# The up products of the first layer's last two token blocks as one Strassen pair, with their weight sums prepared from block 1 on

## The chip, the cores and the metric

The kernel runs on one core of a Trainium2 chip. The metric is device time in microseconds (us) of one execution, the median over runs. The kernel before takes 1470.53 us (three runs, 1470.46 to 1470.94). All operands lie in HBM in float32 and the output is float32. A core has five engines: TensorE (PE, matrix products into PSUM), VectorE (DVE), ScalarE (ACT), GpSimd (POOL) and SyncE (SP), which here issues nearly all DMA transfers. Each engine works through its own instructions in the order in which they were written.

## The reference, cut to what matters

```python
kv  = einsum('bhsd,bhse->bhde', k, v)            # B, H, S, D = 8, 8, 576, 64
o   = einsum('bhsd,bhde->bhse', q, kv)           # no softmax
x   = o / sqrt(mean(o*o, -1) + 1e-6) * g_norm    # -> 4608 tokens x 512

h   = maximum(maximum(x @ w1, x @ w2), x @ w3)   # first layer: 512 -> 768
x   = h @ w_out                                  # 768 -> 512

xn  = x / sqrt(mean(x*x, -1) + 1e-6) * rms_g     # second layer
g   = xn @ w_gate                                # 512 -> 1536
out = (g * sigmoid(g) * (xn @ w_val)) @ w_out2   # 1536 -> 512
```

## The kernel before

**Numbers.** A float32 operand is kept as two parts, hi (rounded to the fast fp32r format) and lo (the rest), and each product is three matmuls, hi x hi, hi x lo and lo x hi, of 128 rows against 512 tokens. Every operand is made so first: hi by ACT (a copy), lo by DVE or POOL (a subtraction).

**Tiles.** The 4608 tokens are nine blocks of 512 (`TB`), a block four token groups (`NS`), and the 512 features four slices of 128 (`KC`). The first layer has six hidden columns of 128 (`J1`), the second twelve (`J2`).

**Order.** The start, up to block 1, follows a written list (`ORDER`). After it the program is loops: for each block `t` and hidden column `j`, `do_p` makes the three up products of the column (each four slices of three matmuls; the maximum is taken by ACT, DVE, DVE), and `do_o` the column's down product (`acc`). Between them stands `slot()`: it runs the work planned for this slot with `at(n, fn)`, a step of the last block's norm (`flush`), a step of the sums of a token pair (`aside`), and one step of the weight preparation (`prep`). The attention of the block ahead is cut into steps as well (`token`: po, sq, ss, pw, xn, pt, hi, lo), five slots to a token group. `pt` is a transpose on PE, and it reads what `xn` on DVE wrote.

**Second layer.** Block 0 is computed directly (`do_gv`, then `do_o`). Blocks 1 to 8 go as four pairs, each by Strassen's scheme in Winograd's form: seven products in the place of eight (`run_unit`, `down`). It needs sums of weight quarters and of token quarters. The weight sums are made in blocks 2 to 8 by 18 `Prep`s, each of 15 steps, from the raw 64-bit words over a float conversion (`conv_a`, `sign`, `conv_bits`, lines 108 to 119) and the sums (lines 209 to 212) to hi and lo (`ws`); four tiles of each are stored to HBM (`wd`), to be loaded again later. `pair_sums` does the same for a pair's tokens (`td`).

**Pools.** `unit` takes one of 38 tiles of 128 x 1024 values: weights, hidden columns and everything in preparation; `room` limits how many of them the preparation may hold (`live`). `psum` takes one of four PSUM banks (`ps`), and `acc` one of four others (`pa`).

Of the kernel before, what the change touches and what calls it, by code (L numbers as in the profile page):

```python
# [20 lines left out]
P = 128  # L21
# [38 lines left out]
def tile_kernel(ctx: ExitStack, tc, qT, k, v, kvt0, kvt1, w1, w2, w3, wo, wg, wv, wo2, out):  # L60
# [97 lines left out]
    class Prep:  # L158

        def __init__(self, i, jp):
# [12 lines left out]
        def step(self):  # L175
            need, fn = self.steps[self.n]
            if live[0] + need > room[0] and need > 0:
                return
            live[0] += need
            if fn:  # L180
                fn()
            self.n += 1

        def load(self, i, jp):
            self.tt, self.g = [], []
# [46 lines left out]

    preps = []
    wait = []

    def prep():
# [5 lines left out]
        if wait and (not preps or len(preps) < 2 and preps[-1].n >= 8) and live[0] + 2 <= room[0]:  # L242
# [17 lines left out]
    def load_kv_part(b, c, only=None):  # L260
        r = b * S
        m, tail = KV.setdefault(b, ([None] * 4, []))
        if c == 2:
# [9 lines left out]
            else:  # L273
                for i, src in enumerate((k, v)):
                    tail.append(rp.tile([P, 512], F32, tag="raw", name="kvt")[:64])
# [83 lines left out]
    def token_steps(i, pool=ps):  # L359
# [42 lines left out]
        def hi():  # L402
            if i // NS not in X:
                new_x(i // NS)
            nc.scalar.activation(X[i // NS][:, 0, :, cut_of(i)], st["pt"], AF.Copy, scale=gc)

        def lo():
            x = X[i // NS]
            f = cut_of(i)
            nc.vector.scalar_tensor_tensor(x[:, 1, :, f], st["pt"], gc, f32(x[:, 0, :, f]), ALU.mult, ALU.subtract)  # L410
# [388 lines left out]
    def slot():  # L799
# [3 lines left out]
        if not side or n_slot[0] % 2:  # L803
            prep()

# [243 lines left out]
    with tc.manual_schedule():  # L1049
# [36 lines left out]
        for word in ORDER.split():  # L1086
# [53 lines left out]
        wait += [Prep(i, jp) for jp in range(J2 // 2) for i in range(3)]  # L1140
        for j in range(J1 - 1):
# [6 lines left out]
        for t in range(2, NB):  # L1148
            last = t + 1 == NB
            if not last:  # L1150
# [7 lines left out]
                if t + 2 < NB:  # L1158
                    at(19, lambda i=base // 2 + 2: load_q(i))
# [4 lines left out]
            else:  # L1164
                at(3, lambda: new_x(NB))
                for c in range(KC):
                    at(4 * c, lambda c=c: load_x2(c))
                    at(4 * c + 4, lambda c=c: hi_x2(c))
                    at(4 * c + 5, lambda c=c: lo_x2(c))
            for j in range(J1):  # L1170
# [8 lines left out]
                if last and j > 2:  # L1179
                    load_w2(j - 3)  # L1180
                if last and j == 3:
                    load_wo2(0)
                slot()
        while preps or wait:
            slot()


        xb = None
        for j in range(J2):
            if j % 2 == 0 and j + 2 < J2:  # L1190
                load_wo2(j // 2 + 1)
            if j + 3 < J2:
                load_w2(j + 3)
# [4 lines left out]
            do_gv(NB, j, slot)  # L1198
            slot()
            if j == 0:  # L1200
                do_o(1, NB - 1, J1 - 1, J1)
# [78 lines left out]
```

## Time and profile before

| | |
|---|---|
| time, median of three runs | 1470.53 us (1470.46 to 1470.94) |
| the profiled execution's own time | 1469.55 us |
| its span, first instruction to last | 1467.4 us |
| PE busy, matmuls | 1459.8 us, 99% of the span, 7262 matmuls |
| DVE, ACT, POOL busy | 62%, 42%, 29% of the span |
| DMA moved | 316.16 MB, a mean of 215 GB/s |

The page cuts the span into 40 slices; PE is at nine tenths or more in each but the first. The chain that ended last is followed back from the last instruction, at each step to what released it; its shares say which engine set the end.

### The profile page before, as it was taken

What the parts mean: (1) busy time and instruction counts of PE and PEld (TensorE: products, weight loads), DVE (VectorE), ACT (ScalarE), POOL (GpSimd) and SP (SyncE); (2) the same over time, 40 slices, a digit from 0 to 9 for tenths busy, and PEclk for the clock granted to TensorE, in tenths of its full rate; (3) what the DMA queues carried; (4) which work ended last, traced back from release to release, by engine and by line L of the source; (5) the groups of instructions that cost most, each with busy time, mean ns of one, the idle gap of its engine ahead of it and who ended that gap; (6) DMA issues with size and microseconds to landing.
All of it is one profiled execution on the core that took longest, in us unless ns stands there. A gap on an engine that the chain in (4) does not pass through costs nothing.

```text
span 1467.4 us, 19952 instructions
## 1 busy us (share of the span) xinstructions
PE 1459.8 (99%) x7262; PEld 1214.7 (83%) x7262; DVE 908.5 (62%) x1377; ACT 620.2 (42%) x1095; POOL 425.3 (29%) x311
## 2 busy tenths in 40 slices
PE   8999999999999999999999999999999999999999
PEld 8888888888888888888888888888888888888887
DVE  6863566676677757752445475674765655754756
ACT  6863354445453545442224342343343442433422
POOL 3212222222231213211232332632424422433323
PEclk9999999999999999999999999999999999999999
DMA  9421435565556662749687654784757843775542
GB/s 362 156 93 58 138 129 194 194 243 210 193 208 251 223 236 108 259 176 391 221 295 269 233 192 173 292 333 152 278 198 275 309 188 149 287 289 198 187 175 105
DMA packets 107218, 316.16 MB, mean 215 GB/s; under 512 B 12977, under 2 KB 13233, under 8 KB 107121
## 3 DMA queue, kind: packets, MB, share of 16 engines
q1 hardware_dynamic: 99200, 302.95, 55.6%
q10 hardware_dynamic: 7920, 11.95, 2.5%
q8 instruction: 57, 0.93, 0.3%
q14 instruction: 41, 0.33, 0.1%
HBM read 241.44 MB, written 73.42 MB: 215 GB/s over the span
## 4 chain that ended last, share of the span: by engine, by line
PE 98%; DMA 1%; SPq 0%; issue 0%; DVE 0%
PE ua L808 18%; PE p L431 10%; PE p L433 10%; PE p L432 10%; PE ub L808 9%; PE da L808 9%; PE db L808 4%; PE uc L808 4%; PE acc L431 4%; PE acc L432 4%; PE acc L433 4%; PE dc L808 2%; PE po L372 2%; PE pk L323 1%; PE pt L400 1%; DMA kvt<-in_kvt 1%
## 5 line engine op out<-in xcount | busy, mean ns | idle before, releaser
L431 PE MATMUL p<-x,w 128*128 128x512 f32 (+1 forms) x656 | 258.1, 393 | 0.0
L433 PE MATMUL p<-x,w 128*128 128x512 f32 (+1 forms) x656 | 254.0, 387 | 0.0
L432 PE MATMUL p<-x,w 128*128 128x512 f32 (+1 forms) x656 | 253.7, 387 | 0.0
L808 PE MATMUL ua<-xo,w 128*128 128x512 f32 x864 | 213.4, 389 | 0.0
L808 PEld LDWEIGHTS ua<-xo,w 128*128 128x128 f32 x864 | 162.2, 188 | 33.7
L450 POOL TENSOR_TENSOR ho<-sl,ho 128x512 fp32r<-128x512 f32 x72 | 97.7, 1364 | 303.9 <-issue 263.6
L450 POOL TENSOR_TENSOR ho<-t,ho 128x512 fp32r<-128x512 f32 x96 | 123.8, 1293 | 132.7 <-ACT ho L449 118.2
L450 POOL TENSOR_TENSOR hs<-h,hs 128x512 fp32r<-128x512 f32 x45 | 67.6, 1502 | 315.2 <-ACT hs L449 295.2
L808 PE MATMUL ub<-xo,w 128*128 128x512 f32 x576 | 146.2, 389 | 0.0
L433 PEld LDWEIGHTS p<-x,w 128*128 128x128 f32 x656 | 123.2, 188 | 25.6
L431 PEld LDWEIGHTS p<-x,w 128*128 128x128 f32 x656 | 123.3, 188 | 24.0 <-issue 0.3
L432 PEld LDWEIGHTS p<-x,w 128*128 128x128 f32 x656 | 123.4, 188 | 23.7
L808 PEld LDWEIGHTS ub<-xo,w 128*128 128x128 f32 x576 | 108.1, 188 | 22.4
L890 ACT ACTIVATE s<-ua 128x512 f32<-128x512 f32 x96 | 57.1, 595 | 139.4 <-PE ua L808 139.1
L808 PE MATMUL da<-ho,wd 128*128 128x512 f32 x432 | 105.7, 389 | 0.0
L449 ACT ACTIVATE ho<-t 128x512 fp32r<-128x512 f32 x96 | 59.4, 627 | 100.5 <-DVE t L641 100.5
L391 POOL TENSOR_TENSOR rs<-ms,mhalf 128x8 f32<-128x8 f32 x36 | 64.6, 1807 | 116.4 <-DVE ms L387 111.5
L462 DVE TENSOR_TENSOR s<-p,s 128x512 f32<-128x512 f32 x45 | 31.1, 691 | 105.5 <-PE p L433 100.4
L808 PEld LDWEIGHTS da<-ho,wd 128*128 128x128 f32 x432 | 81.1, 188 | 16.8
L449 ACT ACTIVATE hs<-h 128x512 fp32r<-128x512 f32 x45 | 28.4, 632 | 139.4 <-DVE h L466 134.5
L431 PE MATMUL acc<-hs,w 128*128 128x512 f32 x216 | 85.4, 395 | 0.0
L838 DVE TENSOR_TENSOR c<-uc,s 128x512 f32<-128x512 f32 x48 | 33.1, 690 | 84.1 <-PE uc L808 83.9
(152 smaller groups left out, 2731.6 us busy)
## 6 DMA issues: line engine op xcount, KB each, us to landing
w<-wd SPq DMA_DIRECT2D x180, 512.0 KB, 7.6
wd<-ws SPq DMA_DIRECT2D x72, 512.0 KB, 3.0
wd<-wd SPq DMA_DIRECT2D x72, 512.0 KB, 7.1
wq<-wd SPq DMA_DIRECT2D x72, 256.0 KB, 8.1
xo<-td SPq DMA_DIRECT2D x32, 512.0 KB, 9.7
q<-in_qT SPq DMA_DIRECT2D x18, 512.0 KB, 6.1
raw<-in_w SPq DMA_DIRECT2D x18, 512.0 KB, 10.1
raw<-in_wo SPq DMA_DIRECT2D x18, 512.0 KB, 6.4
```

Source lines behind the costliest of these rows:

```text
L323: nc.tensor.matmul(pk[h * D:(h + 1) * D, hp, :], kk, vv, start=(c == 0 and hp in ((0, NP // 2) if b == 0 else (0,))), stop=(c == 4), skip_ ...
L372: nc.tensor.matmul(po[:n, f], q[:, hp, o:o + n], kvbd[b][:, hp, :], start=True, stop=True)
L391: nc.gpsimd.tensor_tensor(st["rs"], st["ms"], mhalf.to_broadcast([P, H]), ALU.pow)
L431: nc.tensor.matmul(o, ah, bh, start=first, stop=False)
L432: nc.tensor.matmul(o, ah, bl, start=False, stop=False)
L433: nc.tensor.matmul(o, al, bh, start=False, stop=last)
L449: nc.scalar.activation(hs[:, 0], h, AF.Copy)
L450: nc.gpsimd.tensor_tensor(hs[:, 1], h, f32(hs[:, 0]), ALU.subtract)
L462: nc.vector.tensor_tensor(s2, p, s1, ALU.max)
L808: nc.tensor.matmul(o, aa, bb, start=first and q == 0, stop=last and q == 2, skip_group_check=True)
L838: nc.vector.tensor_tensor(t, p, s, ALU.add)
L890: nc.scalar.activation(t, p, AF.Copy)
```

## The change

The up products of blocks 7 and 8 of the first layer, which were made one block at a time (6 columns x 3 products x 12 matmuls for each block), are made together: the two blocks and the two halves of the features form a 2 x 2 matrix of tokens, and for each of the three up weights columns `j` and `j + 3` form the other. Nine units (`up_unit`) of seven products, six matmuls each, take their place. Around them:

- `Sums`: nine preparations that form the weight sums of the first layer from weights already in SBUF and store them (`sd`). They wait in the same list as the `Prep`s, ahead of them, and begin at the end of block 1, with room for four tiles.
- `prep()` may hold three preparations at once (`depth`, `lead`), looks ahead at the tiles that a preparation will need (`peak`), and is run a second time in every other slot of blocks 2 to 6 (`fast`).
- `tokens_ahead`: in blocks 5 and 6 the attention of blocks 6, 7 and 8 is made early; then the token sums of the pair (`full`, `x_diff`, `x_hi`, `x_lo`).
- `out_down`, `in_down`: the six down weights of the first layer go to HBM and come back, so that their tiles are free meanwhile.
- `Sring`: the weight sums are loaded again, three ahead and then two for each unit.
- `down7` and `down8` make the down products of the two blocks, one block after the other, and layer 2's block 0 follows with two preparation steps a slot (`twice`) and a wait for weights not yet stored (`ready`).

The diff, cut to its core:

```diff
+        lead = 15, 8, 5
         def step(self):
             need, fn = self.steps[self.n]
-            if live[0] + need > room[0] and need > 0:
+            if self.n == 4 and n_slot[0] < self.loaded + 5:
+                return
+            if need > 0 and live[0] + need + (0 if self is preps[0] else preps[0].peak()) > room[0]:
                 return
...
+    class Sums(Prep):
+        lead = 7, 3, 2
+        def __init__(self, i, j):
+            self.n, self.key, self.g, self.loaded = 0, (i, j), [], -9
+            self.steps = [
+                (2, self.fulls), (0, None), (-1, self.diffs), (1, lambda: self.up(0)), (1, lambda: (self.down(0), self.up(1))),
+                (-2, lambda: (self.out(0), self.down(1))), (-1, lambda: self.out(1)),
+            ]
+        def fulls(self):
+            i, j = self.key
+            self.f, self.c = unit([P, 2, 512], F32, "wt"), unit([P, 2, 2, 256], F32, "wt")
+            for n in range(2):
+                w = W[1, i, j + 3 * n]
+                nc.vector.tensor_tensor(self.f[:, n], f32(w[:, 0]), f32(w[:, 1]), ALU.add)
+        def diffs(self):
...
+            nc.vector.tensor_tensor(c0[:, 0], a21, a22, ALU.add)
+            nc.vector.tensor_tensor(c0[:, 1], c0[:, 0], a11, ALU.subtract)
+            nc.vector.tensor_tensor(c1[:, 0], a11, a21, ALU.subtract)
+            nc.vector.tensor_tensor(c1[:, 1], a12, c0[:, 1], ALU.subtract)
+        def up(self, n):
+            self.g.append(unit([P, 2, 2, 256], F32R, "ws"))
+            nc.scalar.activation(self.g[n][:, :, 0], self.c[:, n], AF.Copy)
+        def down(self, n):
+            g = self.g[n]
+            nc.vector.tensor_tensor(g[:, :, 1], self.c[:, n], f32(g[:, :, 0]), ALU.subtract)
+        def out(self, n):
...
+            nc.sync.dma_start(d, f32(self.g[n]))
...
-        if wait and (not preps or len(preps) < 2 and preps[-1].n >= 8) and live[0] + 2 <= room[0]:
+        if wait and not hold[0] and (not preps or len(preps) < depth[0] and preps[-1].n >= preps[-1].lead[depth[0] - 1]) and live[0] + 2 + (preps[0].peak() if preps else 0) <= room[0]:
...
             prep()
+        if fast[0] and not side and n_slot[0] % 2:
+            prep()
...
+        wait += [Sums(i, j) for j in range(J1 // 2) for i in range(3)]
+        room[0], depth[0] = 4, 3
         def pumped():
             tick()
             flush()
+            prep()
...
+        def quarter(u, c, p, s=None):
...
+                    nc.scalar.activation(r, p, AF.Copy)
+                else:
+                    add(p, s, r)
+                return
+            r = R[j, c]
+            if s is not None:
+                p = add(p, s, tmp("c"))
+            nc.vector.tensor_tensor(r, p, r, ALU.max)
+            if i == 2:
...
+                defer(lambda: HT.__setitem__(key, split_h(r, "hs")), 1)
...
+        def up_unit(i, j, between=None):
...
+            b = psum([P, TB], "vb")
+            up1(u, 5, b, True)
+            s5 = copy("s5", b)
+            half_slot()
+            if between is None:
+                c11()
+            up1(u, 6, a)
+            s2 = copy("s2", a)
+            sr.load()
+            half_slot()
+            up1(u, 3, b)
+            quarter(u, 1, b, s2)
+            half_slot()
+            if last1():
+                half_slot()
+            up1(u, 7, a)
+            quarter(u, 3, a, s5)
+            sr.load()
+            half_slot()
+            prev1.append(u)
...
+        depth[0], fast[0] = 3, True
-        for t in range(2, NB):
+        for t in range(2, PA):
...
+                tokens_ahead(t)
...
+        for j in range(J1 // 2):
+            for i in range(3):
...
+                if (i, j) == (1, 0):
+                    room[0], depth[0] = 8, 2
+                if (i, j) == (2, 1):
+                    for n in range(3):
+                        in_down(n)
+                if (i, j) == (0, 2):
+                    for n in range(3, J1):
+                        in_down(n)
+                if (i, j) == (1, 2):
+                    load_w2(0)
+                if (i, j) == (2, 2):
+                    load_w2(1)
                     load_wo2(0)
...
+                up_unit(i, j, between)
...
+            down7(n, n == 0, n == J1 - 1)
...
+            down8(c)
```

How the instructions stand is shown at two places. The first is DVE in block 2. Of the kernel before, from the norm's second `q` rows (`q <- q`, line 541) to the `xn` that a transpose waits for; `ws` and `wt` are tiles of a `Prep`:

```order
L227 TENSOR_TENSOR ws<-wt,ws 128x2x256
L108 TENSOR_SCALAR wt<-raw 128x512
L385 TENSOR_REDUCE ss<-sq 128x8
L387 TENSOR_SCALAR ms<-ss 128x8
L549 TENSOR_TENSOR two<-q,two 128x512
L227 TENSOR_TENSOR ws<-wt,ws 128x2x256
L108 TENSOR_SCALAR wt<-raw 128x512
L227 TENSOR_TENSOR ws<-wt,ws 128x2x256
L118 TENSOR_SCALAR wt<-wt 128x512
L119 ISA wt<-wt 128x1024
L462 TENSOR_TENSOR s_1997<-p_1984,s_1973 128x512
L349 TENSOR_TENSOR xn<-po,rs 128x512
```

The same place of the changed kernel, its end, from `two` to the same `xn` (now line 401); L265 to L268 are the four lines of `diffs`, and L276 is the lo part of a sum:

```order
L610 TENSOR_TENSOR two<-q,two 128x512
L265 TENSOR_TENSOR wt<-wt 128x256
L266 TENSOR_TENSOR wt<-wt 128x256
L267 TENSOR_TENSOR wt<-wt 128x256
L268 TENSOR_TENSOR wt<-wt 128x256
L276 TENSOR_TENSOR ws<-wt,ws 128x2x256
L265 TENSOR_TENSOR wt<-wt 128x256
L266 TENSOR_TENSOR wt<-wt 128x256
L267 TENSOR_TENSOR wt<-wt 128x256
L268 TENSOR_TENSOR wt<-wt 128x256
L276 TENSOR_TENSOR ws<-wt,ws 128x2x256 x2
L523 TENSOR_TENSOR s_2091<-p_2078,s_2059 128x512
L401 TENSOR_TENSOR xn<-po,rs 128x512
```

Ahead of this piece, between the `h` of the column before and `two`, stand one more group L265 to L268, one more L276 and four `fulls` (L260, `wt <- w`, in two pairs), besides `x`, two `q`, `ss` and `ms`, which are the same in both kernels. So from that `h` to this `xn` the changed kernel has 4 `fulls`, 12 `diffs` and 4 `ws` where the one before had 3 `ws` and the four conversions L108 (two), L118 and L119.

The second place is SP's queue of transfers while blocks 7 and 8 are in work. Of the kernel before, in block 7, where the token sums of blocks 5 and 6 are stored (`td`, from the tiles `th`, `b` and `y`); `raw` is a load of raw weights:

```order
L231 DMA wd<-ws 128x1024
L658 DMA td<-th 128x512
L659 DMA td<-b 128x512
L658 DMA td<-th 128x512
L659 DMA td<-y 128x512
L231 DMA wd<-ws 128x1024
L102 DMA raw<-in_wo 128x1024 x2
```

Of the changed kernel, in the same work on blocks 5 and 6, now in the middle of the nine units (line 1263 is `Sring`'s load, 1416 the load of `in_down`, 240 the store of a `Prep`):

```order
L1263 DMA w<-sd 128x1024 x2
L719 DMA td<-th 128x512
L720 DMA td<-b 128x512
L1416 DMA w<-od 128x1024 x3
L719 DMA td<-th 128x512
L720 DMA td<-y 128x512
L240 DMA wd<-ws 128x1024
L1263 DMA w<-sd 128x1024
```

The preparation and the token sums store as before, and the loads of the weight sums and of the down weights now stand in the same queue between them.

## Rows read from the trace of the kernel before

**Rows 1.** The page: the span, and each engine's busy time with its share and instructions.

```profile
span 1467.4 us, 19952 instructions
...
PE 1459.8 (99%) x7262; PEld 1214.7 (83%) x7262; DVE 908.5 (62%) x1377; ACT 620.2 (42%) x1095; POOL 425.3 (29%) x311
```

**Rows 2.** The page: the chain that ended last, shares of the span by engine.

```profile
PE 98%; DMA 1%; SPq 0%; issue 0%; DVE 0%
```

**Rows 3.** PE's waits in the whole span: us in total, times, longest.

```profile
PE busy L298 <- POOL mhalf L1053: 1.4, 1, 1.4
PE pt L400 <- DVE xn L349: 1.2, 3, 0.7
PE pk L323 <- DMA kvt<-in_kvt: 0.8, 1, 0.8
PE po L372 <- ACT kvbd L332: 0.7, 1, 0.7
```

**Rows 4.** The same chain in order of time, Strassen pairs: start us, us, what.

```profile
788.18 1.36 PE ub L808 x6
789.54 1.36 PE uc L808 x6
```

**Rows 5.** Timeline of DVE in block 2: start us, us, line, operation, [idle before <-releaser].

```profile
191.69 0.69 DVE L466 TENSOR_TENSOR h<-p,s 128x512 f32<-128x512 f32 x1 [4.59 <-PE p L433]
...
192.96 2.38 DVE L541 TENSOR_TENSOR q<-q 128x512 f32<-128x512 f32 x2
195.26 0.68 DVE L227 TENSOR_TENSOR ws<-wt,ws 128x512 fp32r<-128x512 f32 x1
195.86 0.41 DVE L108 TENSOR_SCALAR wt<-raw 128x512 f32<-128x512 f32 x1
...
198.21 0.42 DVE L108 TENSOR_SCALAR wt<-raw 128x512 f32<-128x512 f32 x1
...
199.14 0.41 DVE L118 TENSOR_SCALAR wt<-wt 128x512 int32<-128x512 int32 x1
199.59 0.69 DVE L119 CUSTOM_DVE_ANT_0 wt<-wt 128x1024 uint16<-128x1024 uint16 x1
201.18 0.69 DVE L462 TENSOR_TENSOR s<-p,s 128x512 f32<-128x512 f32 x1 [0.89 <-ACT wt L114]
201.78 0.68 DVE L349 TENSOR_TENSOR xn<-po,rs 128x512 f32<-128x512 f32 x1
...
206.16 0.42 DVE L209 TENSOR_TENSOR wt<-wt 128x256 f32<-128x256 f32 x1
206.61 0.43 DVE L210 TENSOR_TENSOR wt<-wt 128x256 f32<-128x256 f32 x1
206.96 0.42 DVE L211 TENSOR_TENSOR wt<-wt 128x256 f32<-128x256 f32 x1
```

**Rows 6.** The chain in the same stretch: the transpose that reads the last xn.

```profile
204.29 0.44 PE pt L400 x4
```

**Rows 7.** Timeline of POOL in the same stretch.

```profile
193.12 1.66 POOL L450 TENSOR_TENSOR hs<-h,hs 128x512 fp32r<-128x512 f32 x1 [10.21 <-ACT hs L449]
197.22 1.95 POOL L391 TENSOR_TENSOR rs<-ms,mhalf 128x8 f32<-128x8 f32 x1 [2.43 <-DVE ms L387]
```

**Rows 8.** Busy us (instructions) of PE, PEld, DVE, ACT, POOL; clock, DMA share, GB/s.

```profile
130.00:630.00 500.00, 500.00 (x2725) 416.52 (x2724) 335.86 (x565) 234.51 (x420) 119.72 (x75) 1.00 0.54 193
```

**Rows 9.** The same columns, three stretches of 10 us at full DMA share.

```profile
660.00:670.00 10.00, 10.00 (x46) 8.29 (x45) 1.98 (x3) 1.23 (x2) 1.29 (x1) 1.00 1.03 415
730.00:740.00 10.00, 10.00 (x45) 8.26 (x45) 7.91 (x8) 1.83 (x4) 4.92 (x4) 1.00 1.03 388
780.00:790.00 10.00, 10.00 (x46) 8.29 (x45) 3.96 (x6) 4.65 (x8) 0.00 (x0) 1.00 1.02 366
```

**Rows 10.** DMA issues: tiles, queue, count, KB each, median us from issue to landing.

```profile
w<-wd SPq DMA_DIRECT2D x180, 512.0 KB, 7.6
wd<-ws SPq DMA_DIRECT2D x72, 512.0 KB, 3.0
```

More of the change, by code (lines that the diff above doesn't have):

```diff
@@ L182, in step, with peak @@
             self.n += 1
+        def peak(self):
+            have = [sum(x for x, _ in self.steps[self.n:n + 1]) for n in range(self.n, len(self.steps))]
+            return max(have + [0])
         def load(self, i, jp):
+            self.loaded = n_slot[0]
             self.tt, self.g = [], []
@@ new lines, in x_units, with __init__, load @@
+        def x_units():
+            X[PA] = [unit([P, 2, TB], F32R, "x") for _ in range(KC)]
+        class Sring:
+            def __init__(self):
+                self.todo = [(i, j, g) for j in range(J1 // 2) for i in range(3) for g in (1, 2)]
+                self.have = {}
+            def load(self):
+                if self.todo:
+                    key = self.todo.pop(0)
+                    w = self.have[key] = unit([P, 2, 2, 256], F32R, "w")
+                    nc.sync.dma_start(f32(w), sd[key])
@@ new lines, in tile_kernel, with half_slot, last1, down7 @@
+        n_half = [0]
+        def half_slot():
+            n_half[0] += 1
+            if n_half[0] % 2:
+                tick()
+            else:
+                slot()
+        prev1 = []
+        def last1():
+            if prev1:
+                u = prev1.pop()
+                up1(u, 4, u["a"])
+                quarter(u, 2, u["a"])
+                return True
+        DA = {}
+        def down7(j, first=False, last=False):
+            if first:
+                DA[PA] = [pa.tile([P, DM], F32, tag="acc", name="acc") for _ in range(NS)]
+            h, w = HT.pop((PA, j)), W[1, "o", j]
+            for c in range(KC):
+                f = slice(c * P, (c + 1) * P)
+                mm3(DA[PA][c], w[:, 0, f], w[:, 1, f], h[:, 0], h[:, 1], first, last)
@@ new lines, in down8 @@
+        def down8(c):
+            d = psum([P, DM], "acc8")
+            f = slice(c * P, (c + 1) * P)
+            for j in range(J1):
+                h, w = HT[PB, j], W[1, "o", j]
+                mm3(d, w[:, 0, f], w[:, 1, f], h[:, 0], h[:, 1], j == 0, j == J1 - 1)
+            if c % 2 == 0:
+                DA["u"] = unit([P, 2, TB], F32, "y8")
+            y = DA["u"][:, c % 2]
+            DA.setdefault(PB, []).append(y)
+            nc.scalar.activation(y, d, AF.Copy)
+        od = {}
@@ L1209, in tile_kernel @@
                 slot()
+            if j == 1:
+                load_x(1)
             if j == 2:
```

219 lines of the change are left out of this document (197 added, 22 removed).

## The prediction

> **What bounds the kernel now.** I read the page's busy shares first, then the chain, then PE's waits, and only then the engines beside PE. The span is 1467.4 us, and PE's matmuls alone are busy for 1459.8 of it [rows 1]. The chain that ended last runs through PE for 98%; DMA has 1%, all of it at the start [rows 2]. PE's waits that are listed come to 4.1 us, none longer than 1.4 [rows 3]. So after the start PE never stands still, and time leaves this kernel only with matmuls. Nothing else can gain; DVE, ACT, POOL and the transfers can only lose, by making PE wait. The profiled execution took 1469.55 us, 2.15 outside its span, and lies 0.98 under the median of 1470.53. I sum the changes against the profiled execution and add 0.98 at the end.
>
> **Removed.** A product of six matmuls stands in the chain with 1.36 us, one behind the other [rows 4], which is 226.7 ns a matmul. Before, blocks 7 and 8 had 2 x 6 x 3 x 12 = 432 up matmuls. After, nine units of seven products of six make 378. The down products stay (6 x 12 and 4 x 18 groups of three as before, only in another order), and no other matmul is added. So 54 x 226.7 ns = **12.2 us** leave PE. This term is sure. It is the whole gain, and the rest of the sum is what PE newly waits for.
>
> **Added on DVE in block 2 (the weight sums).** Here the order shows 4 `fulls`, 12 `diffs` and one more `ws` between an `h` and the `xn` that a transpose on PE waits for. What stands there has little slack. From its timeline, `h` starts at 191.69 and `xn` ends at 201.78 + 0.68 = 202.46 [rows 5]; the transpose that reads it starts at 204.29 [rows 6]. Slack: 1.83 us. Prices: operations of 512 columns start 0.60 apart when back to back (201.18 to 201.78, 195.26 to 195.86), although each is listed with 0.68; those of 256 columns start 0.45 and 0.35 apart (206.16, 206.61, 206.96), so four of them in a group take about 1.48 [rows 5]. Added: 5 x 0.60 + 3 x 1.48 = 7.4 us. Gone from there: two L108 (0.33 each between starts), L118 and L119 (1.06 together), and the 0.89 of idle time for ACT's `wt` [rows 5], together 2.6. DVE comes 4.8 us later to `xn`, 3.0 more than the slack: **3.0 us** of waiting on PE, at the transpose.
>
> The bounds of this term come from the same rows. Two `q` rows took 2.38 us in the place of 1.2, beside POOL's `hs` from 193.12 to 194.78, while a `two` and a `ws` beside POOL's `rs` (197.22 to 199.17) kept their pitch [rows 5, 7]. If two of the added operations meet such a POOL operation, 5.2 us are lost; if one group of `diffs` finds idle time that I have not seen, 2.0. Less than nothing cannot be, since a wait of zero is the best there is: at best the whole 4.8 fits, if PE comes later to that transpose itself. I take 3.0, since the pitch of most rows is the undisturbed one. The Trainium skill ("SBUF — State Buffer", section "Who interferes with whom") says that a VectorE operation with two inputs in SBUF and a GpSimd operation share a pair of ports, and that whoever has them locks the other out. The two slow `q` agree with that, the unhindered `two` and `ws` do not; by the rule alone the term would be the 5.2. `fulls` and `diffs` all read two SBUF operands.
>
> The second place a `Sums` could hurt, its `ws` on ACT, costs nothing: ACT is at 234.51 of 500 us there [rows 8] and `xn` does not wait for it.
>
> **Added on the DMA queue (the nine units).** In this stage the loads of the weight sums stand in SP's queue among the `Prep` stores, the raw loads, the stores of the token sums and the six loads of `in_down`. I counted by the order what is queued from the third product-group of unit 4, where the queue first stays behind, to the load that product 3 of unit 8 reads (the sixteenth of 18): 22 transfers of 512 KB and, with `b`, `td` and the four `xn` stores, 18 of 256 KB, 16.25 MB. In that stretch PE has 27.4 products, 27.4 x 1.36 = 37.3 us. Three stretches of full DMA share moved 415, 388 and 366 GB/s [rows 9]. I take 395, between the mean of all three, 390, and that of the upper two, 401; the bytes then take 41.1 us. A store alone lands 3.0 us after its issue, its median [rows 10], of which 524,288 B at 395 GB/s are 1.3, so 1.7 are added at the end. 41.1 + 1.7 - 37.3 = **5.5 us**, waited for at the `vb` product with the sums of unit 8. At 415 GB/s it is 3.6, at 366 it is 8.8. At best it is nothing, if the queue is not behind when the stretch begins (less cannot be, PE did not wait there before); at worst the 8.8. I take 5.5. This is the least sure term: it is a difference of two sums of some 40 us. Each load is issued 9.5 to 10.9 us ahead of its use, a little more than the 7.6 that a `w` load takes at its median [rows 10]. That cover is what the queue uses up.
>
> **DVE in the nine units.** The last six units (42 products, 57.1 us of PE) give DVE 101 operations: quarters, token sums of the pair, `Prep`s. In the busy stretch before, 565 operations took 335.86 us, 0.594 each [rows 8], so 60.0 us, 2.9 over. This lies beside the queue's 5.5 and is covered by it: while PE waits for a load, DVE catches up. Without that cover it would be at most 2.9, less what four PSUM banks let DVE stay behind (about three products, 4 us). I take nothing.
>
> **Moved at no price.** The token steps of blocks 6 to 8 come earlier with the same instructions, beside the same matmuls. The weights' round trip (`out_down`, `in_down`) adds 12 transfers of 512 KB; those out stand in block 6, where the mean is half a share [rows 8], and those back are in the sum above. In layer 2's block 0 `twice` runs the rest of the `Prep`s. From the last `down8` group to the loads of the tenth hidden column the queue has 52 transfers of 512 KB, 27.3 MB, for 55 products, 74.9 us: 69.0 + 1.7 at 395 GB/s, 4 us to spare.
>
> **Sum.** 1469.55 - 12.2 + 3.0 + 5.5 = 1465.8; with 0.98, **1466.7 us** for the median, 0.26% faster.
>
> **The rivals.**
>
> *Nothing waits.* `xn` and the loads come in time, as 12 `diffs` might fit into idle times of DVE and the queue might not be behind before unit 4. 1470.53 - 12.2 = 1458.3. For it: DVE is idle for a third of the busy stretch and DMA for half [rows 8]. Against: these are means, and the `xn` had 1.83 us of slack for 4.8.
>
> *The waits add up to the gain.* POOL meets DVE in block 2 (5.2), the queue costs 5.5, and DVE's 2.9 is not covered because the two do not fall together. 13.6 - 12.2 = +1.4: 1471.9, no change. For it: every term is of a size that the rows show. Against: PE's waits give DVE time.
>
> *Slower: the queue's rate.* One mechanism, the transfers of the stage in one queue, and a rate at the low end of what was seen. At 360 GB/s the nine units wait 45.1 + 1.7 - 37.3 = 9.5 us, and the tenth column of block 0 waits as well, 75.8 + 1.7 - 74.9 = 2.6; with the 3.0 in block 2 that is 15.1, 2.9 more than the gain. From about 360 GB/s down it decides; at 355 it is 10.2 + 3.7 + 3.0 = 16.9, so 1475.2. For it: stores and loads mix here, and one of three stretches of full share shows 366. Against: the other two show 388 and 415 [rows 9]. The Trainium skill ("DMA: Bandwidth & Descriptors", section "Where 436 GB/s comes from") says that about 358 GB/s of HBM per core bind a transfer between HBM and SBUF, and 435 the fabric. All three stretches were above its 358, so the trace disagrees; at 358 the case would give 1474.2.
>
> **How the numbers follow.** This kernel's measurement cannot tell less than 0.2%, 2.9 us, from no change. The forecast has 42%, with an own range of 1462 to 1471 (waits of 4 to 13 us, the lower bounds of one term with the middle of the other and the reverse); nothing waits 20%; the waits add up 22%; the slow queue 16%. Faster by over 0.2% is below 1467.6: the whole of the 20, and of the 42 the part below, a little over half of its range, six tenths or 26; together 46%. Slower by over 0.2% is above 1473.4: the 16, and 5 of the 22 for waits that add up to more than I found, 21%. The rest, 33%, lies within. The range takes in the first rival, whose time no mechanism here can better, and leaves out of the last what lies above 1474, with the 5 some 17%: 1458 to 1474.
>
> **What would show it.** The product 226.7 ns a matmul must stay, and PE's busy time fall by 12 us. PE's waits should show two new entries: a transpose (`pt`) waiting for `xn` in block 2, some 3 us, and a `vb` or `va` product waiting for DMA `w<-sd` in the later units, some 5. If the second shows instead a release by DVE (a PSUM bank, `quarter` or `s`), DVE's lag was the bound. If `pg` or `pv` wait for `w<-wd` in block 0, the third rival is at work. I am wrong altogether if PE's busy time does not fall by 12, or if waits of over 5 us stand at a place that I counted as free, in blocks 5 and 6 above all, where the attention of three blocks is drawn together.

## The result and the profile after

The changed kernel takes **1487.02 us** (three runs, 1486.95 to 1487.12), the kernel before 1470.53: 16.5 us or 1.1% slower, ratio 1.0111 (95% interval 1.0088 to 1.0134). The forecast was 1466.7, with a range of 1458 to 1474; it was wrong in sign. The profiled execution took 1487.02 us, its span is 1485.2.

The head of the page and PE's waits of the changed kernel, to be held against [rows 1, 3]; the waits are the total, the times and the longest, in us:

```profile
span 1485.2 us, 20182 instructions
PE 1457.9 (98%) x7208; PEld 1208.4 (81%) x7208; DVE 977.8 (66%) x1504; ACT 649.6 (44%) x1155; POOL 437.2 (29%) x319
```

```profile
PE va L871 <- ACT s L953: 8.3, 4, 4.8
PE pt L452 <- DVE xn L401: 4.4, 5, 2.7
PE pr L593 <- ACT two L606: 3.4, 1, 3.4
PE pr L594 <- DVE two L610: 2.9, 1, 2.9
PE busy L350 <- POOL mhalf L1116: 1.4, 1, 1.4
PE va L871 <- DVE c L901: 1.2, 1, 1.2
```

The 54 matmuls are gone (7262 to 7208), yet PE is busy only 1.9 us less, not 12.2, and it waits at three new places. Three marks on PE cut the span: the first `va` product, where the nine units begin, the first `pg`, where layer 2's block 0 begins, and the first `ua`, where the pairs begin. The profile's rows by tile give the start of the first and of the last; the fourth row is the kernel before:

```profile
L871 PE MATMUL va<-x,w x54: 389/389/396, 551.4 to 642.7; 128*128 128x512 f32 x54
...
L492 PEld LDWEIGHTS pg<-x,w x48: 187/188/188, 686.4 to 786.9; 128*128 128x128 f32 x48
...
L871 PEld LDWEIGHTS ua<-xo,w x864: 187/188/188, 796.0 to 1461.0; 128*128 128x128 f32 x173
...
L808 PE MATMUL ua<-xo,w x864: 389/389/397, 778.5 to 1443.3; 128*128 128x512 f32 x173
```

(The matmuls follow their weight loads by 0.2 us: 686.6 and 796.2.) From `va` to `pg` stand 536 matmuls (378 of the units, 156 down products and two of a norm), 121.5 us at 226.7 ns; they took 135.2. From `pg` to `ua` stand 436, 98.8 us; they took 109.6. From `ua` to the end of the span it is 689.0 us, before 688.9. So this is the account of the 17.8 us that the span grew:

| place | us |
|---|---|
| 54 matmuls | -12.2 |
| block 2, weight sums | +4.4 |
| the nine units and the down products behind | +13.7 |
| layer 2's block 0 | +10.8 |
| a wait of 0.5 in block 5, and the rest | +1.1 |

**Block 2.** PE and DVE there; compare [rows 5, 6]:

```profile
204.66 0.39 PE L494 MATMUL p<-x,w 128*128 128x512 f32 x1
207.76 0.85 PE L452 MATMUL pt<-ident,xn 128*128 128x128 f32 x4 [2.71 <-DVE xn L401]
208.27 0.78 PE L492 MATMUL acc<-hs,w 128*128 128x512 f32 x1
208.84 0.63 PE L493 MATMUL acc<-hs,w 128*128 128x512 f32 x1
209.27 0.63 PE L494 MATMUL acc<-hs,w 128*128 128x512 f32 x1
```

```profile
192.24 0.69 DVE L527 TENSOR_TENSOR h<-p,s 128x512 f32<-128x512 f32 x1 [2.79 <-PE p L494]
...
206.43 0.68 DVE L523 TENSOR_TENSOR s<-p,s 128x512 f32<-128x512 f32 x1
207.03 0.68 DVE L401 TENSOR_TENSOR xn<-po,rs 128x512 f32<-128x512 f32 x1
```

The `xn` ends at 207.71, and the transpose waits 2.71 us. Behind it the matmuls start 0.43 apart, not 0.227: PE runs at the lower of its two levels, 1.2 GHz, until about 211.4 (the mean granted clock is 0.81 from 205 to 210 us, and 1.00 from 200 to 205). The 12 `acc` products take 4.3 us (208.27 to 212.61) in the place of 2.7. A wait of 2.7 us cost 4.4.

**The nine units.** Busy us (instructions) of PE, PEld, DVE, ACT and POOL, the granted clock, DMA share and GB/s:

```profile
580.00:590.00 10.00, 9.79 (x44) 7.77 (x43) 9.69 (x13) 5.62 (x12) 3.75 (x3) 1.00 0.36 129
590.00:600.00 10.00, 8.25 (x37) 6.52 (x36) 9.73 (x17) 5.30 (x9) 1.34 (x1) 1.00 0.86 305
...
610.00:620.00 10.00, 8.36 (x36) 6.23 (x34) 9.93 (x14) 7.52 (x14) 3.16 (x2) 1.00 1.01 388
620.00:630.00 10.00, 5.29 (x17) 4.23 (x18) 9.28 (x18) 3.85 (x8) 1.28 (x1) 0.83 1.03 405
```

DVE is busy throughout and PE is not. The longest wait there, from PE's side, ACT's, DVE's and POOL's timelines (start, us, the operation, in brackets the idle time before it and what ended it):

```profile
624.71 2.92 PE L871 MATMUL va<-xs,w 128*128 128x512 f32 x6 [4.82 <-ACT s L953]
```

```profile
623.54 0.63 ACT L510 ACTIVATE hs<-r 128x512 fp32r<-128x512 f32 x1 [3.45 <-DVE r L1343]
624.07 0.58 ACT L953 ACTIVATE s<-va 128x512 f32<-128x512 f32 x1
```

```profile
614.03 1.79 DVE L236 TENSOR_TENSOR ws<-wt,ws 128x512 fp32r<-128x512 f32 x1
...
618.60 1.79 DVE L702 TENSOR_TENSOR b<-b,y 128x512 f32<-128x512 f32 x1
...
622.75 0.69 DVE L1343 TENSOR_TENSOR r<-c,r 128x512 f32<-128x512 f32 x1
...
624.41 1.65 DVE L119 CUSTOM_DVE_ANT_0 wt<-wt 128x1024 uint16<-128x1024 uint16 x1
```

```profile
613.65 1.61 POOL L511 TENSOR_TENSOR hs<-r,hs 128x512 fp32r<-128x512 f32 x1 [17.96 <-ACT hs L510]
618.29 1.55 POOL L511 TENSOR_TENSOR hs<-r,hs 128x512 fp32r<-128x512 f32 x1 [3.03 <-ACT hs L510]
624.24 1.28 POOL L511 TENSOR_TENSOR hs<-r,hs 128x512 fp32r<-128x512 f32 x1 [4.41 <-ACT hs L510]
```

Read from the bottom: POOL's `hs` meets an operation of DVE and stretches it (10 of the 11 `hs` between 575 and 655 us do, seven by 1.0 to 1.1 us and three by 0.6 to 0.7, 9.3 us in all); DVE comes late to `r`; ACT stands, in order, at an `hs` that reads it; and the copy `s` that would free `va` stands behind that `hs`. No product here waits for a load of `sd`, and from 575 to 625 us DVE is busy for 47.8 of 50 us and waits 1.1 us for transfers.

**Layer 2's block 0.** ACT, DVE and PE:

```profile
724.63 0.64 ACT L617 ACTIVATE q<-y 128x512 f32<-128x512 f32 x1 [0.83 <-DMA xn<-y]
726.55 0.63 ACT L615 ACTIVATE y<-y 128x512 f32<-128x512 f32 x1 [1.29 <-DMA xn<-y]
...
728.15 0.58 ACT L542 ACTIVATE sg<-pg 128x512 f32<-128x512 f32 x1
730.82 0.63 ACT L606 ACTIVATE two<-q 128x512 fp32r<-128x512 f32 x1 [2.08 <-DVE q L602]
```

```profile
732.81 0.43 DVE L118 TENSOR_SCALAR wt<-wt 128x512 int32<-128x512 int32 x1 [1.68 <-ACT wt L205]
...
734.48 0.68 DVE L610 TENSOR_TENSOR two<-q,two 128x512 fp32r<-128x512 f32 x1
```

```profile
731.50 0.79 PE L593 MATMUL pr<-two,ones 128*128 128x512 f32 x1 [3.45 <-ACT two L606]
735.21 0.80 PE L594 MATMUL pr<-two,ones 128*128 128x512 f32 x1 [2.92 <-DVE two L610]
735.81 0.63 PE L492 MATMUL pv<-x,w 128*128 128x512 f32 x1
```

Block 8's norm waits on ACT for tiles that block 7's `xn` stores still hold; their transfers stand in a queue at full share (409 and 399 GB/s from 720 to 740). The second `two` is late on DVE: it stands behind a conversion (L118) that waits 1.68 us for a preparation's step on ACT. PE, in order, stops at the norm's product `pr`, twice, and after it the clock is down again (a mean of 0.52 from 730 to 740).

### The profile page after: what moved, and what is told of

Same layout as the page of the kernel before. It is cut to its first block, busy times and chain, and to the rows that moved or that the text cites. A ratio compares the mean times of both kernels' runs of the same rounds, so it can differ in the third digit from the quotient of the medians.

```text
span 1485.2 us, 20182 instructions
## 1 busy us (share of the span) xinstructions
PE 1457.9 (98%) x7208; PEld 1208.4 (81%) x7208; DVE 977.8 (66%) x1504; ACT 649.6 (44%) x1155; POOL 437.2 (29%) x319
## 4 chain that ended last, share of the span: by engine, by line
PE 89%; DVE 4%; DMA 4%; issue 2%; ACT 1%; POOL 1%; SPq 0%; ACTq 0%; DVEq 0%; POOLq 0%
PE ua L871 18%; PE ub L871 9%; PE da L871 9%; PE p L492 8%; PE p L494 7%; PE p L493 7%; PE db L871 4%; PE uc L871 4%; PE acc L493 4%; PE acc L492 4%; PE acc L494 4%; PE dc L871 2%; PE po L424 2%; PE va L871 1%; PE pk L375 1%
## 5 line engine op out<-in xcount | busy, mean ns | idle before, releaser
L492 PE MATMUL p<-x,w 128*128 128x512 f32 (+1 forms) x512 | 201.8, 394 | 0.0
L494 PE MATMUL p<-x,w 128*128 128x512 f32 (+1 forms) x512 | 198.0, 387 | 0.0
L493 PE MATMUL p<-x,w 128*128 128x512 f32 (+1 forms) x512 | 197.7, 386 | 0.0
L494 PEld LDWEIGHTS p<-x,w 128*128 128x128 f32 x512 | 96.1, 188 | 19.9
L511 POOL TENSOR_TENSOR hs<-h,hs 128x512 fp32r<-128x512 f32 x33 | 50.9, 1541 | 207.8 <-ACT hs L510 196.8
L492 PEld LDWEIGHTS p<-x,w 128*128 128x128 f32 x512 | 96.3, 188 | 18.5 <-issue 0.2
L493 PEld LDWEIGHTS p<-x,w 128*128 128x128 f32 x512 | 96.3, 188 | 18.2
L492 PE MATMUL acc<-hs,w 128*128 128x512 f32 x216 | 86.2, 399 | 0.0
L494 PE MATMUL acc<-hs,w 128*128 128x512 f32 x216 | 84.7, 392 | 0.0
L493 PE MATMUL acc<-hs,w 128*128 128x512 f32 x216 | 84.6, 392 | 0.0
```

What stands on the lines that cost most here:

```text
L492: nc.tensor.matmul(o, ah, bh, start=first, stop=False)
L493: nc.tensor.matmul(o, ah, bl, start=False, stop=False)
L494: nc.tensor.matmul(o, al, bh, start=False, stop=last)
L511: nc.gpsimd.tensor_tensor(hs[:, 1], h, f32(hs[:, 0]), ALU.subtract)
```

## The experiments

All times are set against a run of the kernel before on the same chip (1469.8 to 1471.8 us). The changed kernel itself stands at +16.5 us. Units is first `va` to first `pg`, block 0 first `pg` to first `ua`, pairs first `ua` to the end of the span. The runs e1 to e11 are single ones, e12 has four, e13 seven. In e4 every engine had the instructions of the changed kernel in the same order, so its row shows how far the columns move by themselves: 1.2 us in the units, 1.7 in block 0.

| run | us | against before | units | block 0 | pairs |
|---|---|---|---|---|---|
| after | 1487.02 | +16.5 | 135.2 | 109.6 | 689.0 |
| e1_two_sums | 1484.38 | +12.6 | 135.9 | 111.5 | 688.9 |
| e2_lo_on_dve | 1489.32 | +17.6 | 138.7 | 109.7 | 688.8 |
| e3_no_prep_in_units | 1533.51 | +61.8 | 124.4 | 167.5 | 688.9 |
| e4_norm_later | 1488.44 | +16.7 | 136.4 | 111.3 | 689.1 |
| e5_norm_gap | 1484.58 | +14.8 | 136.1 | 107.2 | 689.1 |
| e6_hs_later | 1486.39 | +16.6 | 134.4 | 111.0 | 688.9 |
| e7_sums_late | 1486.49 | +16.7 | 127.6 | 109.0 | 698.3 |
| e8_all | 1483.57 | +13.8 | 126.9 | 109.6 | 697.9 |
| e9_late | 1503.47 | +33.4 | 127.6 | 107.1 | 720.5 |
| e10_more_prep | 1515.84 | +45.7 | 148.0 | 99.1 | 720.3 |
| e11_spread | 1480.93 | +10.9 | 123.8 | 102.3 | 706.0 |
| e12_early_diffs | 1485.13 | +15.0 | 123.8 | 103.9 | 710.5 |
| e13_lo_on_pool | 1465.83 | -4.3 | 123.8 | 102.1 | 690.9 |

**e1_two_sums: fewer weight sums at a time.**

```diff
-        room[0], depth[0] = 4, 3
+        room[0], depth[0] = 4, 2
...
-        depth[0], fast[0] = 3, True
+        depth[0], fast[0] = 2, True
         for t in range(2, PA):
+            if t == 3:
+                depth[0] = 3
```

> At most two Sums at a time in blocks 1 and 2 in the place of three. Theory (DVE's operations between one h and the next xn set the wait in block 2): 4 fulls, 8 diffs and 3 ws stand there, so DVE is 4 x 0.60 + 2 x 1.48 - 2.6 = 2.8 us later than before, 1.0 more than the slack of 1.83; the wait falls from 2.71 us to about 1.0, too short for the clock to fall, and block 2 loses 1 us in the place of the 4.8 measured from idle time and slow matmuls. Time: 1487.0 - 3.8 = 1483, if the later start of the layer-2 preparations costs nothing. Rival (the transpose waits for something else, ACT or the slow POOL pow): the wait stays above 2 us and the time at 1486 to 1488.

PE's waits for `xn`:

```profile
PE pt L452 <- DVE xn L401: 2.1, 4, 0.9
```

The longest is 0.9 where 1.0 was worked out, the granted clock stays at 1.00 from 200 to 215 us, and the time falls by 3.9 against before. Block 2 was DVE's operations ahead of one `xn`, as forecast, and the slow matmuls behind the wait were some two fifths of its price (1.7 of 4.4).

**e2_lo_on_dve: the lo parts of `hs` in the units on DVE.**

```diff
-                defer(lambda: HT.__setitem__(key, split_h(r, "hs")), 1)
+                defer(lambda: HT.__setitem__(key, split_h(r, "hs", nc.vector)), 1)
```

> The lo parts of the 18 hidden columns of blocks 7 and 8 are subtracted by DVE (0.60 us each) and not by POOL. Theory A (POOL's subtraction locks DVE out of the ports for about 1.05 us): 8 of the 11 such POOL operations in the nine units stretched a DVE operation, 8.4 us; DVE gets 11 x 0.60 = 6.6 more of its own, so the nine units change by -2 to 0 us: 1485 to 1487. Theory B (the stretched operations are chance, DVE simply has too many operations): DVE gets 6.6 to 10.8 us more to do and PE waits for it: 1492 to 1498.

The stretch grows by 3.5 us, between the two theories, and neither comes out. The changed kernel and this run from first `va` to first `pg` (the columns as above), and a wait of DVE in this run:

```profile
551.40:686.60 135.20, 125.48 (x538) 101.10 (x538) 108.55 (x170) 75.54 (x137) 26.04 (x18) 0.99 0.73 278
...
550.30:689.00 138.70, 126.62 (x537) 101.74 (x536) 107.06 (x182) 75.41 (x137) 9.66 (x6) 0.98 0.72 271
...
DVE hs L511 <- ACT hs L510: 8.5, 12, 0.8
```

The edit moves 12 subtractions, not 18: DVE has 12 operations more, 12 x 0.60 = 7.2 us, and yet is busy for 1.5 us less. So the meetings with POOL had cost DVE some 8.7 us, close to the 9.3 counted in the rows (of 10 operations, not of 8). What ate the gain is order: each lo part on DVE stands right behind its hi part on ACT, and DVE waits about 0.7 us for it, 8.5 in all. The run prices the meetings; what the stretch would take without them it does not show. Since the edit adds no transfer, it does show that what stands in DVE's order moves the stretch.

**e3_no_prep_in_units: no preparation in the units.**

```diff
-                if (i, j) == (0, 0):
-                    hold[0] = False
...
         last1()
+        hold[0] = False
         new_x(NB)
```

> No layer-2 preparation runs in the nine units; the four that did so (26 us of DVE by their rows) run in layer 2's block 0. Theory (DVE's load is what PE waits for in the units, not the queue of transfers and not the order on ACT): from the first va product to the first pg product PE takes 121.5 us of matmuls and loses at most 3, where it took 135.2. Rival (the loads of the weight sums, or ACT's copies behind an hs that waits for its r): the stretch still takes over 130 us. Layer 2's block 0 gets four preparations more and is already at full DMA share, so the whole time may rise: 1475 if block 0 takes them, 1495 if not.

The marks of this run:

```profile
L871 PE MATMUL va<-x,w x54: 388/389/393, 550.9 to 631.8; 128*128 128x512 f32 x54
...
L492 PEld LDWEIGHTS pg<-x,w x48: 187/188/333, 675.0 to 833.6; 128*128 128x128 f32 x48
```

The stretch takes 124.4 us, 2.9 over the matmuls alone: 10.8 of the 13.7 were the four preparations. The preparations use DVE and the queue of transfers alike; that PE's waits in the changed kernel end with ACT and DVE, that DVE there hardly waits for transfers, and that e2 lengthens the stretch without one, puts it down to DVE. Block 0 then took 58 us more than in the changed kernel, with 49.6 us of waits at `acc` for ACT's `gs`; the work cannot simply be put there.

**e4_norm_later and e5_norm_gap: block 8's norm.**

```diff
-            if j == 0:
-                norm.append(end1_steps(PB, DA[PB]))
+            if j == 2:
+                norm.append(end1_steps(PB, DA[PB]))
```

> Block 8's norm begins two hidden columns of layer 2 later (j = 2 in the place of j = 0). Theory (its first copies on ACT wait for y tiles that block 7's four xn stores still hold, and gs, sg and two stand behind them on ACT): the waits of pr, 3.4 and 2.9 us, and the slow clock after them go away; layer 2's block 0 loses under 3 us in the place of 10.6, the time is about 1479. Rival (the queue of transfers is full there and PE would wait for w<-wd in any case): pg or pv wait for w<-wd in their place, and the time is 1484 to 1488.

Nothing moved: PE's two waits at `pr` were 3.9 and 2.9 us at the same place, since the norm's steps stand behind those of block 7 in `norm` and the order of all instructions came out the same. The run tells nothing of the theory. The next puts empty steps ahead of it:

```diff
-                norm.append(end1_steps(PB, DA[PB]))
+                norm.append(gap(3, end1_steps(PB, DA[PB])))
```

> Three empty slots stand ahead of block 8's norm, so that it starts after block 7's xn stores have landed. (Starting it two columns later had moved nothing, since it queues behind block 7's norm in any case.) Theory (y tiles held by stores that land late in a full queue hold up ACT, and gs, sg and two behind): pr's two waits, 3.4 and 2.9 us, and the slow clock after them go; the stretch from the first pg to the first ua product, 109.6 us, falls to 100 to 102, and the time to 8 us above the kernel before in the place of 16.5. Rival (DVE and ACT are late there through the two preparation steps a slot, wherever the norm stands): pr still waits over 3 us, and the time is 14 to 18 above before.

The first wait of `pr` goes, the second stays with 1.9, and 2.0 us of waiting for `gs` come up: 2.4 us gained of the 8 expected. Even that is not sure: in e8, with the same gap, block 0 takes 109.6, and the runs with neither the gap nor less to do there spread from 109.0 to 111.5. The held `y` tiles were at most one of several things that were late.

**e6_hs_later: the split of `hs` put off.**

```diff
-                defer(lambda: HT.__setitem__(key, split_h(r, "hs")), 1)
+                defer(lambda: HT.__setitem__(key, split_h(r, "hs")), 3)
```

> The split of a finished hidden column into hs is put off by three half slots in the place of one. Theory A (in the units DVE is late, and PE feels it early because ACT, in order, stands at an hs that waits for its r while the copy s of a va product stands behind it): PE's waits at va for ACT, 8.3 us, fall by half or more, and the stretch from the first va to the first pg product, 135.2 us, falls to 128 to 131; the time is 10 to 13 us above before. Theory B (DVE's load alone counts, the order on ACT does not): the waits move to DVE's c or r, and the stretch stays at 134 to 136.

The waits at `va` for ACT fall from 8.3 to 5.8, but the stretch by 0.8 only, less than it moved in e4. ACT's order hands DVE's lateness on; it isn't its cause.

**e7_sums_late and e8_all: the token sums of blocks 5 and 6 out of the units.** The tokens come from HBM in one tile, and a generator in the down products ahead of the pair makes hi, the differences in place, and lo:

```diff
-        if t and t % 2 == 0:
+        if t and t % 2 == 0 and t != 6:
...
+    def build_late(n):
...
+        sub(b12, b11, b11)
+        lo(3, b22, g)
+        yield
+        hi(5, b11)
+        sub(b22, b12, b12)
```

> The token sums of blocks 5 and 6 are no longer made in the nine units; they are made from the blocks' tokens in the second pair's last down products, straight into their tiles, without the way over HBM. The units lose 16 DVE operations (9.6 us), 8 on ACT and 20 transfers of 256 KB, and a preparation step may run in each slot where it ran in every other one. Theory (DVE's load sets the units): the stretch from the first va to the first pg product falls from 135.2 to between 126 and 131 us, and the time to 8 to 12 us above before, if the pairs hold the 16 operations without a wait of PE (they would show at xo). Rival (the preparation takes the room at once, with steps in each slot): the stretch stays over 133, and block 0 of layer 2, with less left to prepare, loses less than 10.6.

> All of these together with two Sums at a time: two Sums, the norm's gap, the later hs, the later token sums. If the three stalls are separate and each edit takes its own away, 16.5 - 3.8 - 8 - 7 = 2 us below before, give or take 3. If they share a cause (a full queue, or preparations that are merely pushed on from place to place), it stays 5 or more above before.

The units fall to 127.6, inside the range; 16 DVE operations, with the 8 on ACT and the 20 transfers that left with them, were worth 7.6 us. The pairs pay it back, 9.3 us, at one place: a difference waits 2.1 us for POOL's lo parts (`xo`), four pairs of DVE's operations beside POOL's take 2.3 to 3.5 us for 1.2, DVE's own work stands behind them, and PE waits 5.4 us at `da`. The sum of the edits comes to 2.7 us where 18.5 were expected.

**e9_late and e10_more_prep: the same sums by way of HBM, in the pairs' up units.**

```diff
+                if n < 2 and ph == 0:
+                    late.append(late_sums(2 * n + 6))
...
             if n_half[0] % 2:
                 tick()
+                if n_half[0] > 16:
+                    prep()
```

(The last two lines only in the second.)

> Two Sums at a time, the norm's gap and the later hs as before; and the token sums of both last pairs (blocks 5 and 6, 7 and 8) leave the nine units and layer 2's block 0. They are made from HBM in the up units of pair 0 and pair 1 and stored for later, so that no down product waits for them (the pairs lost 9 us where the sums stood in one pair's down products, since DVE there waited, in order, for POOL's parts). Theory (each place loses what DVE and the queue cannot take there, and the pairs have room for both): units 126 to 128 us, block 0 at 104 to 107 in the place of 109.6 since 5.2 MB leave its full queue, pairs unchanged within 2 us: 5 to 9 us below the kernel after of the same chip's scale, that is 0 to 6 below before. Rival (load moved is load that stalls elsewhere): the pairs lose 5 or more at ua or ub, and it stays above before.

> As the last, with a preparation step in every half slot of the nine units from the third unit on, so that nearly two more preparations (some 13 us of DVE, 6 MB of transfers) are done before block 0. Theory: DVE in the units has the 9.6 us free that the token sums left, so the units rise from 127 to at most 131 us, and block 0, with 6 MB less in its queue, falls to 100 to 104; together 2 to 5 us faster than the last. Rival (DVE is at its limit already, each operation added in the units is paid in full): units at 137 or more, and no faster than the last.

e9 fails in the pairs, which take 31.5 us more. The largest wait:

```profile
PE da L924 <- ACT op L1071: 11.1, 2, 6.8
```

I read it as the accumulator tile `op` waiting for the tiles of the sums, which are still being stored. The trace agrees: ACT stands twice at `op` until a store `td<-xl` has landed, 23.5 us in all. e10's two halves are clearer than its sum. Of the preparations' 42 DVE operations in block 0 it leaves 4, and block 0 takes 99.1 us, the bare matmuls' 98.8, where e9 took 107.1. The units take 148.0 for the 38 operations, 20.4 us more, for which DVE is busy 18.1 us longer. The same work costs PE 20.4 us in the units and 8.0 in block 0.

**e11_spread, e12_early_diffs, e13_lo_on_pool: the token sums where they fit.** All three have two `Sums` at a time, the gap, the later `hs`, and

```diff
-            if self.n == 4 and n_slot[0] < self.loaded + 5:
+            if self.n == 4 and n_slot[0] < self.loaded + (10 if in_units[0] else 5):
...
         lo(w)
         yield
         yield
+        if t == NB - 1:
+            yield
+            yield
```

and `load_x(1)` ahead of the `down8` products. e11 makes both late pairs' sums with 22 DVE operations in the down products; e12 makes the 8 differences ahead, in the up units, and leaves 8 lo parts to DVE and 6 to POOL; e13 gives all 14 to POOL, in the order in which the units need them, and sets the differences five ticks apart in the place of three:

```diff
-                nc.vector.tensor_tensor(XO[m, k][:, 1], raw[:, q, k], f32(XO[m, k][:, 0]), ALU.subtract)
+                nc.gpsimd.tensor_tensor(XO[m, k][:, 1], raw[:, q, k], f32(XO[m, k][:, 0]), ALU.subtract)
```

> Two Sums at a time, the norm's gap, the later hs; the token sums of both last pairs are made in SBUF in the down products ahead of their pair (with all lo parts on DVE, so that DVE does not wait in order for POOL as in e7_sums_late); a preparation in the units waits ten half slots, not five, for its raw weights before it converts (in e9_late DVE stood 5.7 us at a conversion whose raw load had not landed); two more slots ahead of the product pr of block 8's norm; xr loaded before the down8 products. Theory (only what DVE and the queue cannot take in its place is lost): units 123 to 126, block 0 101 to 105, the pairs within 3 us of 662.6, block 2 about 1 us: 1464 to 1470, 1 to 6 us below before. Rival (the pairs' down products have no room for 22 DVE operations): da waits for DVE's o by 3 us or more in two places, and the slow clock follows: 1475 or more.

> As e11_spread, but the 8 differences of a late pair's tokens are made in place one by one in the up units before, and the down products ahead of the pair hold 8 lo parts on DVE and 6 on POOL (the tokens themselves come once more from HBM, straight into their tiles), where they held 22 operations on DVE. Theory (e11_spread was 5.4 us ahead of the kernel before at the first pair's start and lost 17 in the pairs, in the two places where 22 DVE operations stood in some 25 us): the two waits at da, 4.9 us each, and the slow clock behind them go, the pairs take 689 to 692 us from the first ua product to the end of the span as before the change, and the time is 1464 to 1468, 2 to 6 us below before. Rival (the pairs are at DVE's limit in the up units too): ua or ub waits for DVE's c or ACT's s in their place, and the time stays above 1472.

> As e12_early_diffs, but all 14 lo parts of a late pair's tokens are POOL's, in the order in which the units need them, and DVE has none; the 8 differences stand five ticks apart, not three. Theory A (what made PE wait at da was POOL's operations on SBUF that lock out DVE's: in e12 each pair of DVE's xo rows took 2.4 to 3.5 us beside POOL's and 1.2 without): da waits no more than 0.7, ua or ub at most 2 us for xo, the pairs take 689 to 693 us, and the time is 1464 to 1468, 2 to 6 us below before. Theory B (the down products have no room for these operations on any engine beside PE): POOL's 14 x 1.26 = 17.6 us end late, ua or ub waits for xo by 3 us or more at two places, and the time stays above 1472.

In e11 the units (123.8) and block 0 (102.3) come out as worked out, and the pairs lose 17: `da` waits twice for 4.9 us. Block 0 does so with 54 DVE operations of preparations, where the changed kernel has 42: it has no token sums there, `xr` is loaded earlier, and `pr` stands two slots later and no longer waits. (The 5.7 us that the expectation lays to a raw load ended, in e9's trace, with a store, `DVE wt L108 <- DMA wd<-ws: 5.7`; the raw loads had landed 8 us before.) In e12, 8 operations on DVE do the harm of 22, since POOL's six, and four `ho`, stand beside them. DVE and POOL of e12:

```profile
1107.86 2.45 DVE L830 TENSOR_TENSOR xo<-xr,xo 128x512 fp32r<-128x512 f32 x2
...
1110.84 2.89 DVE L830 TENSOR_TENSOR xo<-xr,xo 128x512 fp32r<-128x512 f32 x2
...
1118.34 3.45 DVE L830 TENSOR_TENSOR xo<-xr,xo 128x512 fp32r<-128x512 f32 x2
```

```profile
1113.14 9.77 POOL L817 TENSOR_TENSOR xo<-xo 128x512 fp32r<-128x512 f32 x6
```

Two such operations take 1.2 us on a free DVE, so the four pairs lose some 6 us, and `da` waits 5.4. And of e13, where DVE has only operations that read PSUM:

```profile
1105.98 0.69 DVE L967 TENSOR_TENSOR o<-dc,op 128x512 f32<-128x512 f32 x1 [0.67 <-PE dc L937]
1107.34 0.69 DVE L967 TENSOR_TENSOR o<-dc,op 128x512 f32<-128x512 f32 x1 [0.67 <-PE dc L937]
...
1108.70 0.69 DVE L967 TENSOR_TENSOR o<-db,op 128x512 f32<-128x512 f32 x1 [0.67 <-PE db L937]
```

```profile
1106.94 2.56 POOL L817 TENSOR_TENSOR xo<-xo 128x512 fp32r<-128x512 f32 x2
1109.45 2.56 POOL L825 TENSOR_TENSOR xo<-xr,xo 128x512 fp32r<-128x512 f32 x2
```

Neither slows the other. The Trainium skill ("SBUF — State Buffer", section "Who interferes with whom") says that the two engines contend only for a shared pair of SBUF ports; these rows agree, with 2.4 to 3.5 us for two operations on SBUF and 0.69 for one on PSUM. e13 takes **1465.83 us** (1464.23 to 1466.84), ratio 0.9971 to before (0.9960 to 0.9983), its mean granted clock is 1.0 and no wait is longer than 1.4. It is faster than both kernels, than the one before by 0.3%. Its last step also lowers DVE's count and spreads the differences, so by itself it does not part the meetings with POOL from the count; e11 against e12, with 22 operations and 8 for the same wait, does.

## Why the prediction was wrong

- **The gain was right.** 54 matmuls left. e13 shows what they are worth where little waits: PE busy 1450.2 us, 9.6 below [rows 1].
- **Block 2 was right as a mechanism and short in its price.** From `h` to the end of `xn` DVE took 15.5 us where it had taken 10.8, 4.7 more; 4.8 were worked out. 3.0 us of waiting were forecast at the transpose, 2.71 came. The slow clock after it, 1.7 more, had no term in the sum, here or at the two other places: PE's busy time fell by 1.9, not by 12.2, so 10.3 us went to slower matmuls and restarts behind waits (2.6 of them stay in e13).
- **The step that failed first is "DVE in the nine units", "I take nothing".** It was mis-sized and wrongly covered. I had priced 101 operations at a mean of 0.594 us, 60.0 in all, which holds few meetings with POOL, and left the 1.1 us that [rows 5, 7] had shown for one `hs` as a bound for block 2 alone. The last six units have 100, but they kept DVE busy for 64.3 us: 7.2 over PE's 57.1 where I had 2.9, with 10 of 11 `hs` in the way. The cover, a wait for the queue, never came, and with the waits in DVE's own order the six units took 69.7 us; from first `va` to first `pg` 13.7 were lost. The prediction's own sign for DVE's lag, a PSUM bank that is freed late where a load was expected, is what PE's waits show, with ACT's `s` as the last link.
- **"Added on the DMA queue", 5.5 us, did not happen.** No product waited for `sd`. The shares of 1.0 with 388 to 405 GB/s at 610 to 630 show the full queue that I had worked out, but PE was behind by then, so the loads were in time. That `va` waited for ACT and DVE, and nowhere for DMA, decides it for this kernel. What the queue would have cost a PE that kept its pace is not shown: the runs in which it nearly did (e3, e11 to e13) have fewer transfers there.
- **"Moved at no price" failed in layer 2's block 0.** I followed the weights there, with "4 us to spare", and they did come in time. What I did not follow was ACT's and DVE's order: two preparation steps a slot, block 7's stores landing late in the full queue, and the norm's `pr` behind them. It cost 10.8 us. Beside the gap and without token sums, fewer preparations took all but 0.3 of it away (e10); with more preparations than here, a `pr` two slots later and `xr` loaded earlier left 3.3 to 3.5 (e11 and e13). How much of it is the queue and how much the order on ACT and DVE stays open.
- **The rivals.** The one on the slower side named a rate below 360 GB/s. The full stretches of 10 us in the units, 600 to 660, show 388 to 415, and no product of the units or of block 0 waits for a load, so its mechanism is refuted, and the time came out slower by another one. "Nothing waits" is refuted by the waits at three places. "The waits add up to the gain" was nearest, with prices of 13.6 in all where 30.0 came: in block 2 the slow clock stood in the place of POOL, the queue's term did not come, and only DVE's in the units was real.

## What to carry to other kernels

A tuned kernel in which PE never waits has its slack in the other engines' order, not in their mean busy share; work that is moved should be priced at each place with what stands beside it, and first of all with POOL's operations on SBUF beside DVE's. Take operations off the engine that is late there, space them, or give them to POOL where DVE reads PSUM: the same change went from +16.5 to -4.3 us by the edits of e13 together, and no run shows what each of them is worth there. And a wait of PE should be priced with the slow matmuls that may follow it.

## What the runs showed of the hardware

- Behind most of PE's longer waits the granted clock fell to its lower level, 1.2 GHz, for some microseconds: matmuls 0.43 apart behind 2.71 us of waiting in block 2, a mean clock of 0.52 from 730 to 740 us behind 3.45 and 2.92. Not behind all: after a wait of 2.97 us in e2 the next six matmuls took 1.67 us, as after one of 1.22 us there (1.66). With no wait above 1.4 (e13) the mean was 1.0.
- One POOL subtraction on SBUF of 1.3 to 1.6 us lengthened a DVE operation on SBUF in 10 of 11 cases in the units, by 1.0 to 1.1 us in seven and 0.6 to 0.7 in three; a DVE operation that read PSUM stayed at 0.69 (e13).
- One core alone moved 388 to 415 GB/s between HBM and SBUF in the six stretches of 10 us from 600 to 660 us, with loads and stores mixed. The Trainium skill ("DMA: Bandwidth & Descriptors", section "Where 436 GB/s comes from") gives about 358 per core as what binds; the measurement decides here.
